# Loading the first chunks of an RWKV-7 scan four steps a partition and turning them by products with the identity

## The chip, the core and the metric

The kernel runs on one core of one Trainium2 chip, as one program from the first load to the last store. The metric is the device time of a run in microseconds, as the median of several runs. A profile comes from one execution of its own; its span is measured from the first to the last recorded instruction.

## What is computed

The input are six tensors of 4 batches, 8 heads, 768 steps and a head dimension of 40. The first part is a recurrence over the steps, with a 40 by 40 state for each batch and head; the second is a dense layer pair over the 3072 resulting tokens of 320 elements.

```python
for t in range(S):
    y[:, :, t] = np.einsum('bhd,bhde->bhe', rt, state)
    Sa = np.einsum('bhde,bhe->bhd', state, at)
    state_decay = state * wt[:, :, None, :] - np.einsum('bhd,bhe->bhde', Sa, bt)
    state = state_decay + np.einsum('bhd,bhe->bhde', vt, kt)
...
h = np.maximum(x @ w_in, 0.0)      # 3072x320 by 320x2048
return h * h @ w_out               # 3072x2048 by 2048x320
```

w lies between 0.85 and 0.95. The dense weights arrive as 64-bit floats and are rounded to 32 bits on the chip. Everything else is 32-bit.

## The kernel before

The steps are cut into chunks of 128, so there are 6 chunks for each of 4 batches, 24 in all, worked chunk by chunk with the four batches of a chunk in turn (`order`). Within a chunk the recurrence is written as products of 128 by 128 matrices per head; only the state passes from one chunk to the next. Heads go in pairs: a head's 40 elements lie padded to 64 rows, so that two heads fill 128 partitions and four pairs (`NP`) fill one PSUM bank of 128 by 512.

**Loading.** `fetch` (L139) brings one of w, a, b, k, r, v of one chunk with one DMA: steps on partitions, 8 heads of 40 elements in each, so 1024 pieces of 160 bytes. It lands in a tile [128, 8, 64] of a ring (L116): two tiles for w, four that a and b share, two each for k and for b as `rest` needs it, one for r, three for v. The pads (elements 40 to 63 of each head) are filled once by POOL, with 1.0 for w and 0.0 for the others (L121). `load_early` (L145) fetches w, b, a of a chunk, `load` (L148) k, the kept decays, r, v and b once more. All of them are issued by SyncE (SP).

**Turning.** `turn` (L313) brings a tile to "elements on partitions, steps along the row", four transposes by TensorE into one bank.

**Early part.** `early` (L342) works on what doesn't need the state. It turns w; scans it on DVE up and down from the middle of the chunk (L352, L353: a running product, `data1` being a tile of ones); takes reciprocals (L357, L358); turns b and a; multiplies them by the decays (L364, L365); stores the decays to memory (`kept_e`); and multiplies b by a for each head (`products`, L320: contraction over the 40 rows). The result N, 128 by 128 for each of 8 heads, is copied by ACT from PSUM into one tile of a single buffer (L373, L376, L377; odd heads are put down with their halves exchanged). It is then stored to memory in pieces: four blocks of the diagonal (`kept_q` or `kept_d`), their joins (`kept_m`, first 10 chunks only) and the off-diagonal quarter (`kept_n`). As there is one buffer for N, the next chunk's first copy waits until these stores have been read out.

**Solve.** The unit triangular matrices 1 + N have to be inverted. POOL does so for the small blocks, in units of 1, 1, 2, 2, 2, 2, 2, 4, 4 and 4 chunks: it loads the kept blocks (L420), solves (L448, L450) and stores the result (`kept_t`, L453). `inverses` (L457) loads the blocks back and joins them to whole inverses with small TensorE products (T copied at L484 to L501).

**Rest and chain.** `rest` (L568) turns k, r and v, and makes the products that the chunk's output needs (A, RV, RX; masked by DVE at L332 with `upper`). `chain` (L604) carries the state through: `xr` (L619), solve by T, the output and the new state. The outputs are the tokens of the dense layers.

**The order of work.** A start-up part does `early` for the first four chunks, of which 0 and 1 keep N on the chip (`g`). Then come 24 slots, one for each chunk. In slots 0 to 3 (`woven`, L881) generators are interleaved by hand-set weights: the chain of the slot, the `rest` of the next chunk, the `early` of up to two later chunks (4 and 5, 6 and 7, 8 and 9, then 10), and the rounding of the dense weights (ACT at L258 and L262, DVE at L266 and others). From slot 4 on (`sorted_slot`, L908) the dense layers fill TensorE, beside the `early`s of chunks 11 and later. Each engine runs its instructions in the order in which the program gave them; an instruction that waits holds up all behind it on that engine. SP issues nearly all DMAs in one such order; `store` (L108) puts a store a few steps behind the place where it is called.

Of the kernel before, what the change touches and what calls it, by code (L numbers as in the profile page):

```python
# [8 lines left out]
FP32 = mybir.dt.float32  # L9
I32 = mybir.dt.int32  # L10
U32 = mybir.dt.uint32
Alu = mybir.AluOpType
# [5 lines left out]
def kernel(  # L18
# [70 lines left out]
    def single(name, shape):  # L89
        return const.tile(shape, FP32, tag=name, name=name)  # L90
# [23 lines left out]


    class Ring:  # L116
        def __init__(self, name, n, shape, fill, pads):
            self.tiles = [single(f"{name}{i}", shape) for i in range(n)]
            self.at = -1
            for t_ in self.tiles:  # L120
                nc.gpsimd.memset(pads(t_), fill)  # L121

        def next(self):
            self.at = (self.at + 1) % len(self.tiles)
            return self.tiles[self.at]

    pads = lambda t_: t_[:, :, D:]
    rings = {}
    for nm, n, fill in (("w", 2, 1.0), ("ab", 4, 0.0)):
        rings[nm] = Ring(f"in_{nm}", n, [128, H, DP], fill, pads)  # L130

    def more_rings():
        for nm in ("k", "b", "r", "v"):
            rings[nm] = Ring(f"in_{nm}", {"r": 1, "v": 3}.get(nm, 2), [128, H, DP], 0.0, pads)

    order = [(bb, c) for c in range(NCH) for bb in range(B)]
    loaded, early_loaded = {}, {}

    def fetch(ring, src, i):  # L139
        bb, c = order[i]  # L140
        t_ = rings[ring].next()
        nc.sync.dma_start(out=t_[:, :, :D], in_=src[bb, :, c * C:(c + 1) * C, :].rearrange("h t d -> t h d"))
        return t_

    def load_early(i):  # L145
        early_loaded[i] = {nm: fetch(ring, src, i) for nm, ring, src in (("w", "w", w), ("b", "ab", b), ("a", "ab", a))}

    def load(i, g=None):  # L148
        x_ = loaded[i] = {"k": fetch("k", k, i)}
# [3 lines left out]
        x_["r"] = fetch("r", r, i)  # L153
        later(lambda: x_.update(v=fetch("v", v, i), b=fetch("b", b, i)), 2 if g is not None else 0)

    load_early(0)
    load_early(1)


    ident = single("ident", [128, 128])  # L160
    make_identity(nc, ident)
    ones = single("ones", [128, MID])
    nc.vector.memset(ones, 1.0)
    upper = single("upper", [128, 128])
    nc.gpsimd.memset(upper, 1.0)
    nc.gpsimd.affine_select(out=upper, in_=upper, compare_op=Alu.is_gt, fill=0.0, base=0,
# [134 lines left out]
    FINE = 6  # L301
    SMALL = units[FINE][0]
    kept_q = dram.tile([SMALL, H, 2, 2, Q, Q], FP32, tag="q", name="kept_q")
    kept_m = [dram.tile([2, Q, H, Q], FP32, tag=f"m{i}", name=f"kept_m{i}") for i in range(SMALL)]
    unit_of = {first + n: u for u, (first, nb) in enumerate(units) for n in range(nb)}

    kept_d = [dram.tile([nb, H, 2, Q * (HC + Q)], FP32, tag=f"d{u}", name=f"kept_d{u}") for u, (_, nb) in enumerate(units)]
# [2 lines left out]
    kept_t = [dram.tile([classes(u), nb, H, 2, 2, Q // classes(u), Q] if u < FINE else [classes(u), nb, H, 2, HC // classes(u), HC], FP32,  # L310
                        tag=f"t{u}", name=f"kept_t{u}") for u, (_, nb) in enumerate(units)]

    def turn(x_):  # L313
        p_ = psum(ps_w)
        for q in range(NP):
            nc.tensor.transpose(p_[:, q * 128:(q + 1) * 128], pair(x_, q), ident)  # L316
        return quads(p_)
# [24 lines left out]
    def early(i, g=None, apart=False):  # L342

        x_ = early_loaded.pop(i)
        dec = decays.next() if g is None else kept_here[i]
        if g is not None:
            nc.vector.memset(dec[:, :A_, :, MID:MID + 1], 1.0)
        up, down, aT = (dec[:, n] for n in (UP, DOWN, A_))
        wT = turn(x_["w"])
        yield  # L350
        for q in range(NP):
            nc.vector.tensor_tensor_scan(up[:, q, MID + 1:C + 1], wT[:, q, MID:], ones, 1.0, Alu.mult, Alu.mult)  # L352
            nc.vector.tensor_tensor_scan(down[:, q, MID - 1::-1], wT[:, q, MID - 1::-1], ones, 1.0, Alu.mult, Alu.mult)  # L353
        yield
        if not apart:
            bT_, aT_ = turn(x_["b"]), turn(x_["a"])
        nc.vector.reciprocal(down[:, :, MID + 1:C + 1], up[:, :, MID + 1:C + 1])  # L357
        nc.vector.reciprocal(up[:, :, :MID], down[:, :, :MID])  # L358
        yield
        if apart:  # L360
            bT_, aT_ = turn(x_["b"]), turn(x_["a"])
            yield
        bT = turned("bT", 1)
        nc.vector.tensor_tensor(bT, bT_, down[:, :, 1:C + 1], Alu.mult)  # L364
        nc.vector.tensor_tensor(aT[:, :, :C], aT_, up[:, :, :C], Alu.mult)  # L365
        if g is None:
            store(kept_e[i], dec[:USED])
        yield
        bb, c = order[i]
        t_ = new("N", [128, H, C], 1)  # L370
        for e, p_ in enumerate(products(bT, aT[:, :, :C])):
            plain, flip_ = t_[:, e:NP:2], t_[:, NP + e::2]
            nc.scalar.copy(plain, p_[:, ::2])  # L373
            for half in range(2):
                own_, other = (slice(n * HC, (n + 1) * HC) for n in (half, 1 - half))
                nc.scalar.copy(flip_[own_, :, own_], p_[other, 1::2, other])  # L376
            nc.scalar.copy(flip_[:HC, :, HC:], p_[:HC, 1::2, HC:])  # L377
        joins = lambda half: t_[half * HC:half * HC + Q, :, half * HC + Q:(half + 1) * HC]
        for half in range(2):
            for n in range(2):  # L380
                at = half * HC + n * Q
                if i < SMALL:
                    kept, to = kept_q[i, :, half, n], at + Q
                else:
                    u = unit_of[i]
                    kept, to = kept_d[u][i - units[u][0], :, half], (half + 1) * HC
                    kept = kept[:, n * Q * HC:n * Q * HC + Q * (to - at)].rearrange("h (s t) -> h s t", s=Q)
                store(kept.rearrange("h s t -> s h t"), t_[at:at + Q, :, at:to], 1, nc.scalar if g is not None and n else nc.sync)
            if i < SMALL and g is None:
                store(kept_m[i][half], joins(half), 1)  # L390
        if g is None:
            store(kept_n[i], t_[:HC, :, HC:], 1)
        else:
            g["dec"], g["N"] = dec, new("N21", [HC, H, HC], 2)
            nc.scalar.copy(g["N"], t_[:HC, :, HC:])
            g["joins"] = spare("joins", i)
            for half in range(2):
                nc.scalar.copy(g["joins"][half * HC:half * HC + Q], joins(half))
        yield
# [57 lines left out]
    def inverses(i, g, queue=nc.sync):  # L457
        bb, c = order[i]
        u = unit_of[i]
        kept = kept_t[u][:, i - units[u][0]]  # L460
        g["T"] = T = new("T", [128, H, HC], 2)
        if u >= FINE:
            for col in range(classes(u)):
                queue.dma_start(out=T[col::classes(u)], in_=kept[col].rearrange("h f j t -> (f j) h t"))  # L464
        else:


            blocks = new("blocks", [128, H, Q], 1)
            for col in range(classes(u)):
                queue.dma_start(out=blocks[col::classes(u)], in_=kept[col].rearrange("h f k j t -> (f k j) h t"))  # L470
        if "N" not in g:
            g["N"] = new("N21", [HC, H, HC], 2)
            queue.dma_start(out=g["N"], in_=kept_n[i])
            if u < FINE:
                g["joins"] = spare("joins", i)
                for half in range(2):
                    queue.dma_start(out=g["joins"][half * HC:half * HC + Q], in_=kept_m[i][half])
        if u >= FINE:
            return
        yield  # L480
        upper_ = spare("turned", i)
        nc.vector.transpose(upper_.rearrange("p h t -> p (h t)"), blocks.rearrange("p h t -> p (h t)"))
        for n in range(2):
            nc.scalar.activation(T[:, :, n * Q:(n + 1) * Q], blocks, Act.Copy, scale=which[:, n:n + 1])  # L484
# [31 lines left out]
    def turn_rv(i, g):  # L516
        x_ = g["x"]
        while "v" not in x_:
            line.pop(0)[1]()
        g["rT"], g["vT"] = turned("rT", 2), turned("kvT", 1)  # L520
        p_, p2_ = turn(x_["r"]), turn(x_["v"])
        nc.scalar.copy(g["rT"], p_)  # L522
        nc.scalar.copy(g["vT"], p2_)
        g["v"] = x_["v"]
# [495 lines left out]
```

## Time and profile before

| what | us |
|---|---|
| median of 3 runs | 987.33 (986.18 to 988.89) |
| the profiled execution, its run | 987.0 |
| its span | 985.3 |
| TensorE busy | 875.7 |
| DVE busy | 485.0 |
| POOL busy | 576.1 |
| ACT busy | 275.5 |
| a turn of four transposes, mean of one transpose record | 0.418 |
| a scan of 128x64 | 0.271 |

The engines work beside each other, so their busy times don't add up to the span. PE is TensorE's matmul side and PEld its weight loads; DVE is VectorE, ACT ScalarE, POOL GpSimd, SP SyncE. A line of the views names the engine, the line of the kernel, the operation and its tiles, output first; in brackets stands the idle time ahead of it on its engine, and what ended that. Matmuls of 32-bit floats show as two records each. The clock given is the share of full speed that TensorE was granted. The DMA share is the mean busy share of the core's 16 DMA engines. The page counts 263431 DMA packets for 104.16 MB, of which 246148 are under 512 bytes.

### The profile page before, as it was taken

To read this page: it belongs to the slowest core of one execution; us is meant where nothing else is said; L and a number is where in the kernel's file an instruction comes from. 1 tells how busy PE (TensorE), PEld (TensorE's weight loads), DVE (VectorE), ACT (ScalarE), POOL (GpSimd) and SP (SyncE) were. 2 spreads that over 40 slices of the span, in tenths; PEclk is the share of its full clock that TensorE was granted. 3 is DMA by queue.
4 is the path that set the end of the run, shared out by engine and by line. 5 is a ranking of instruction groups with operands and counts; after the bars stand their busy time and mean duration, and the time that the engine had idled before them with its cause. 6 is when DMAs were issued, how large, how long until landed. Compare 5 with 4: busy or idle time off the path is not lost.

```text
span 985.3 us, 21632 instructions
## 1 busy us (share of the span) xinstructions
PE 875.7 (89%) x8752; PEld 725.8 (74%) x8752; DVE 485.0 (49%) x868; ACT 275.5 (28%) x711; POOL 576.1 (58%) x989
## 2 busy tenths in 40 slices
PE   6447666667897999999999999999999999999998
PEld 4436555556685888888888888888888888887776
DVE  5528775758755454475446655632444423331111
ACT  3132423234323342332223232322222222222111
POOL 4788482836018985999976999959999800000000
PEclk9757565657698999999999999999999999999999
DMA  8987987894667579465588772585404364030000
GB/s 100 143 160 131 191 158 164 171 170 118 91 127 132 100 138 183 92 122 78 97 167 156 124 113 70 102 183 82 66 19 78 82 121 71 14 64 8 14 13 14
DMA packets 263431, 104.16 MB, mean 106 GB/s; under 512 B 246148, under 2 KB 252676, under 8 KB 261924
## 3 DMA queue, kind: packets, MB, share of 16 engines
q1 hardware_dynamic: 259188, 86.39, 50.9%
q0 software_dynamic: 3056, 16.26, 6.9%
q8 instruction: 69, 1.13, 0.5%
q10 hardware_dynamic: 1088, 0.13, 0.1%
q14 instruction: 30, 0.25, 0.1%
HBM read 70.11 MB, written 30.66 MB: 102 GB/s over the span
## 4 chain that ended last, share of the span: by engine, by line
PE 64%; SPq 1%; DVE 1%; DMA 1%; ACT 0%; issue 0%; ACTq 0%
PE ps_f L87 36%; PE ps_w L87 11%; PE ps_c L87 11%; PE ps_w L316 4%; PE ps_c L560 1%; PE ps_c L643 1%; PE ps_w L544 1%; DMA dec<-kept_e 1%; SPq L108 1%; SPq L464 0%; DMA tokens<-tokens 0%; DVE decay L357 0%; DVE state L535 0%; DVE RV L332 0%; ACT N L376 0%
## 5 line engine op out<-in xcount | busy, mean ns | idle before, releaser
L448 POOL TENSOR_TENSOR half_p<-half_n,half_t 128x120 f32<-128x120 f32 (+37 forms) x438 | 255.7, 584 | 84.4 <-DMA half_n<-kept_d 26.5
L450 POOL TENSOR_TENSOR half_t<-half_t,half_p 128x120 f32<-128x120 f32 (+37 forms) x438 | 275.9, 630 | 34.3
L87 PE MATMUL ps_f<-w_out,hid 128*128 128x320 f32 x768 | 217.4, 436 | 0.0
L87 PEld LDWEIGHTS ps_f<-w_out,hid 128*128 128x128 f32 x768 | 142.5, 190 | 54.6 <-issue 0.2
L87 PE MATMUL ps_f<-tokens,w_in 128*128 128x256 f32 x672 | 157.2, 388 | 0.0
L87 PEld LDWEIGHTS ps_f<-tokens,w_in 128*128 128x128 f32 x672 | 126.7, 194 | 17.9 <-issue 1.0
L734 DVE TENSOR_TENSOR hid<-hid 128x512 f32<-128x512 f32 x96 | 88.9, 963 | 50.2 <-ACT hid L727 49.7
L727 ACT ACTIVATE hid<-ps_f 128x512 f32<-128x512 f32 x84 | 50.2, 597 | 96.0 <-PE ps_f L87 96.0
L352 DVE TENSOR_TENSOR_SCAN decay<-ps_w,ones 128x64 f32<-128x64 f32 x88 | 23.8, 271 | 81.5 <-PE ps_w L316 81.5
L669 DVE TENSOR_TENSOR tokens<-ps_c,dec 128x512 f32<-128x512 f32 x24 | 16.5, 688 | 79.3 <-PE ps_c L87 79.3
L87 PE MATMUL ps_w<-decay,bT 40*128 40x128 f32 x352 | 30.0, 308 | 27.0 <-DVE decay L365 27.0
L373 ACT COPY N<-ps_w 128x256 f32<-128x256 f32 x48 | 17.7, 369 | 121.6 <-PE ps_w L87 74.7
L87 PEld LDWEIGHTS ps_w<-decay,bT 40*128 40x128 f32 x352 | 27.6, 213 | 30.2 <-issue 19.1
L510 DVE TENSOR_TENSOR kvT<-ps_w,dec 128x512 f32<-128x512 f32 x24 | 16.5, 688 | 66.9 <-ACT minus_x L630 33.9
L87 PE MATMUL ps_f<-tokens,w_third 64*128 64x256 f32 x336 | 46.9, 385 | 1.5 <-DVE w_out L266 1.5
L332 DVE TENSOR_TENSOR RX<-ps_w,upper 128x512 f32<-128x512 f32 x48 | 30.8, 683 | 32.1 <-PE ps_w L87 31.6
L332 DVE TENSOR_TENSOR RV<-ps_w,upper 128x512 f32<-128x512 f32 x48 | 30.9, 686 | 31.1 <-PE ps_w L87 30.8
L87 PEld LDWEIGHTS ps_c<-xr,T 64*64 64x64 f32 x768 | 30.7, 149 | 20.5 <-issue 15.0
L522 ACT COPY rT<-ps_w 128x512 f32<-128x512 f32 x24 | 14.0, 585 | 108.3 <-PE ps_w L316 108.3
L87 PE MATMUL ps_c<-xr,T 64*64 64x40 f32 x768 | 36.8, 243 | 3.6 <-ACT xr L619 1.6
L357 DVE RECIPROCAL decay<-decay 128x256 f32<-128x256 f32 x22 | 38.2, 1736 | 0.0
L532 DVE TENSOR_TENSOR f<-end,dec 128x4 f32<-128x4 f32 x20 | 5.1, 255 | 66.6 <-DMA dec<-kept_e 66.6
(130 smaller groups left out, 1411.7 us busy)
## 6 DMA issues: line engine op xcount, KB each, us to landing
kept_e<-decay SPq DMA_DIRECT2D x22, 633.8 KB
dec<-kept_e SPq DMA_DIRECT2D x22, 633.8 KB
hid<-in_moe_w_out_dram SPq DMA_DIRECT2D x16, 320.0 KB
half_n<-kept_d POOLq DMA_DIRECT2D x6, 768.0 KB, 10.3
in_w<-in_w_dram SPq DMA_DIRECT2D x24, 160.0 KB
in_ab<-in_b_dram SPq DMA_DIRECT2D x24, 160.0 KB
in_ab<-in_a_dram SPq DMA_DIRECT2D x24, 160.0 KB
in_k<-in_k_dram SPq DMA_DIRECT2D x24, 160.0 KB
```

Source lines behind the costliest of these rows:

```text
L87: nc.tensor.matmul(o, l_, r_, start=start, stop=True, skip_group_check=True)
L316: nc.tensor.transpose(p_[:, q * 128:(q + 1) * 128], pair(x_, q), ident)
L332: nc.vector.tensor_tensor(t_, p_, over4(upper), Alu.mult)
L352: nc.vector.tensor_tensor_scan(up[:, q, MID + 1:C + 1], wT[:, q, MID:], ones, 1.0, Alu.mult, Alu.mult)
L357: nc.vector.reciprocal(down[:, :, MID + 1:C + 1], up[:, :, MID + 1:C + 1])
L373: nc.scalar.copy(plain, p_[:, ::2])
L448: nc.gpsimd.tensor_tensor(p_, part[:, at:at + m_].unsqueeze(1).to_broadcast([128, n, m_]), t3[:, :n, s:s + 1].to_broadcast([128, n, m_]), ...
L450: nc.gpsimd.tensor_tensor(t3[:, :n, s + 1:], t3[:, :n, s + 1:], p_, Alu.subtract)
L510: nc.vector.tensor_tensor(kT, kT_, down[:, :, 1:C + 1], Alu.mult)
L669: nc.vector.tensor_tensor(t_, y_, g["up"][:, :, :C], Alu.mult)
L727: nc.scalar.activation(h_, p_.rearrange("p f t -> p (f t)"), Act.Relu)
L734: nc.vector.tensor_tensor(h_, h_, h_, Alu.mult)
```

## The change

The w, a and b of chunks 0 to 10 and the r of chunks 0 to 4 are fetched in runs. Four consecutive steps of one head are 160 floats in a row in memory; one partition takes such a run for two heads, in pieces of 640 bytes. The 32 runs of a chunk and one pair of heads fill 32 partitions, and the four pairs the 128, with four DMAs for each fetch. Such a tile is turned by eight products with the identity as the moving operand: for each of the four steps in a run and each head of a pair, 64 columns of the tile are the weight, and the 128 results go to every fourth column of the bank. A weight of 64 columns reads 24 elements past its 40; these belong to the next step, or, at the last, to 24 columns filled by POOL (`beyond`). So the pad rows of a turned tile now hold values of another step. For w the scan therefore takes a second operand `least`, with the larger of the running product and `least` as the result: −3e38 in the rows of the head, 1.0 in its pad rows. The whole pads of such a tile are filled by DVE when the tile is first fetched in the old way. The two first fetches of a are issued by ACT. Beside this, N is laid out [128, 2, 8, 64], by halves of its columns, so that `kept_n` and `kept_m` are stored in pieces of 2048 bytes; `kept_m` becomes twice as large, with the half that is read back as before.

```diff
+    RUN = 4
+    RW = RUN * D
+    flat = lambda t_: t_.rearrange("p h d -> p (h d)")
+    beyond = lambda t_: flat(t_)[:, 2 * RW:2 * RW + DP - D]
+    in_runs = {"w": 11, "ab": 11, "r": B + 1}
...
-        def next(self):
+        def next(self, runs_=False):
             self.at = (self.at + 1) % len(self.tiles)
-            return self.tiles[self.at]
+            t_ = self.tiles[self.at]
+            if not runs_ and self.at in self.bare:
+                self.bare.remove(self.at)
+                nc.vector.memset(self.pads(t_), self.fill)
+            return t_
...
-    def fetch(ring, src, i):
+    def fetch(ring, src, i, queue=nc.sync):
         bb, c = order[i]
-        t_ = rings[ring].next()
+        runs_ = i < in_runs.get(ring, 0)
+        t_ = rings[ring].next(runs_)
+        if runs_:
+            for q in range(NP):
+                queue.dma_start(out=flat(t_)[q * C // RUN:(q + 1) * C // RUN, :2 * RW].rearrange("g (e x) -> g e x", e=2),
+                                in_=src[bb, 2 * q:2 * q + 2, c * C:(c + 1) * C, :].rearrange("e (g s) d -> g e (s d)", s=RUN))
+            return t_
...
-    load_early(0)
-    load_early(1)
+    load_early(0, (nc.sync, nc.sync, nc.scalar))
+    load_early(1, (nc.sync, nc.sync, nc.scalar))
...
-    ones = single("ones", [128, MID])
-    nc.vector.memset(ones, 1.0)
+    least = single("least", [128, MID])
+    nc.gpsimd.memset(least, 1.0)
+    for e in range(2):
+        nc.gpsimd.affine_select(out=least[e * DP:(e + 1) * DP], in_=least[e * DP:(e + 1) * DP], compare_op=Alu.is_ge, fill=-3.0e38,
+                                base=-D, pattern=[[0, MID]], channel_multiplier=1)
...
-    kept_m = [dram.tile([2, Q, H, Q], FP32, tag=f"m{i}", name=f"kept_m{i}") for i in range(SMALL)]
+    kept_m = [dram.tile([2, Q, H, HC], FP32, tag=f"m{i}", name=f"kept_m{i}") for i in range(SMALL)]
...
-    def turn(x_):
+    def turn(x_, runs_=False):
         p_ = psum(ps_w)
+        if runs_:
+            by_step = p_.rearrange("d (x s) -> d s x", s=RUN)
+            for n in range(RUN):
+                for e in range(2):
+                    at = e * RW + n * D
+                    mm(by_step[e * DP:(e + 1) * DP, n], flat(x_)[:, at:at + DP], ident, True)
+            return quads(p_)
         for q in range(NP):
             nc.tensor.transpose(p_[:, q * 128:(q + 1) * 128], pair(x_, q), ident)
         return quads(p_)
...
-        wT = turn(x_["w"])
+        wT = turn(x_["w"], i < in_runs["w"])
         yield
         for q in range(NP):
-            nc.vector.tensor_tensor_scan(up[:, q, MID + 1:C + 1], wT[:, q, MID:], ones, 1.0, Alu.mult, Alu.mult)
-            nc.vector.tensor_tensor_scan(down[:, q, MID - 1::-1], wT[:, q, MID - 1::-1], ones, 1.0, Alu.mult, Alu.mult)
+            nc.vector.tensor_tensor_scan(up[:, q, MID + 1:C + 1], wT[:, q, MID:], least, 1.0, Alu.mult, Alu.max)
+            nc.vector.tensor_tensor_scan(down[:, q, MID - 1::-1], wT[:, q, MID - 1::-1], least, 1.0, Alu.mult, Alu.max)
...
-        t_ = new("N", [128, H, C], 1)
+        t_ = new("N", [128, 2, H, HC], 1)
         for e, p_ in enumerate(products(bT, aT[:, :, :C])):
-            plain, flip_ = t_[:, e:NP:2], t_[:, NP + e::2]
-            nc.scalar.copy(plain, p_[:, ::2])
+            plain, flip_ = t_[:, :, e:NP:2], t_[:, :, NP + e::2]
+            nc.scalar.copy(plain, p_[:, ::2].rearrange("s h (f t) -> s f h t", f=2))
...
-        joins = lambda half: t_[half * HC:half * HC + Q, :, half * HC + Q:(half + 1) * HC]
+        joins = lambda half, f=Q: t_[half * HC:half * HC + Q, half, :, f:]
...
-                store(kept_m[i][half], joins(half), 1)
+                store(kept_m[i][half], joins(half, 0), 1)
         if g is None:
-            store(kept_n[i], t_[:HC, :, HC:], 1)
+            store(kept_n[i], t_[:HC, 1], 1)
...
-                    queue.dma_start(out=g["joins"][half * HC:half * HC + Q], in_=kept_m[i][half])
+                    queue.dma_start(out=g["joins"][half * HC:half * HC + Q], in_=kept_m[i][half, :, :, Q:])
...
-        p_, p2_ = turn(x_["r"]), turn(x_["v"])
+        p_, p2_ = turn(x_["r"], i < in_runs["r"]), turn(x_["v"])
```

More of the change, by code (lines that the diff above doesn't have):

```diff
@@ L116, with __init__ @@
     class Ring:
-        def __init__(self, name, n, shape, fill, pads):
+        def __init__(self, name, n, shape, fill, pads, first=None):
             self.tiles = [single(f"{name}{i}", shape) for i in range(n)]
             self.at = -1
+            self.fill, self.pads = fill, pads
+            self.bare = set(range(n)) if first else set()
             for t_ in self.tiles:
-                nc.gpsimd.memset(pads(t_), fill)
-        def next(self):
+                nc.gpsimd.memset((first or pads)(t_), fill)
@@ L128 @@
+    beyond = lambda t_: flat(t_)[:, 2 * RW:2 * RW + DP - D]
+    in_runs = {"w": 11, "ab": 11, "r": B + 1}
     rings = {}
     for nm, n, fill in (("w", 2, 1.0), ("ab", 4, 0.0)):
-        rings[nm] = Ring(f"in_{nm}", n, [128, H, DP], fill, pads)
+        rings[nm] = Ring(f"in_{nm}", n, [128, H, DP], fill, pads, beyond)
     def more_rings():
         for nm in ("k", "b", "r", "v"):
-            rings[nm] = Ring(f"in_{nm}", {"r": 1, "v": 3}.get(nm, 2), [128, H, DP], 0.0, pads)
+            rings[nm] = Ring(f"in_{nm}", {"r": 1, "v": 3}.get(nm, 2), [128, H, DP], 0.0, pads, beyond if nm in in_runs else None)
@@ L142, in fetch, with load_early @@
         nc.sync.dma_start(out=t_[:, :, :D], in_=src[bb, :, c * C:(c + 1) * C, :].rearrange("h t d -> t h d"))
         return t_
-    def load_early(i):
-        early_loaded[i] = {nm: fetch(ring, src, i) for nm, ring, src in (("w", "w", w), ("b", "ab", b), ("a", "ab", a))}
+    def load_early(i, queues=(nc.sync,) * 3):
+        early_loaded[i] = {nm: fetch(ring, src, i, q) for q, (nm, ring, src) in zip(queues, (("w", "w", w), ("b", "ab", b), ("a", "ab", a)))}
     def load(i, g=None):
@@ L348, in early @@
         up, down, aT = (dec[:, n] for n in (UP, DOWN, A_))
-        wT = turn(x_["w"])
+        wT = turn(x_["w"], i < in_runs["w"])
         yield
         for q in range(NP):
-            nc.vector.tensor_tensor_scan(up[:, q, MID + 1:C + 1], wT[:, q, MID:], ones, 1.0, Alu.mult, Alu.mult)
-            nc.vector.tensor_tensor_scan(down[:, q, MID - 1::-1], wT[:, q, MID - 1::-1], ones, 1.0, Alu.mult, Alu.mult)
+            nc.vector.tensor_tensor_scan(up[:, q, MID + 1:C + 1], wT[:, q, MID:], least, 1.0, Alu.mult, Alu.max)
+            nc.vector.tensor_tensor_scan(down[:, q, MID - 1::-1], wT[:, q, MID - 1::-1], least, 1.0, Alu.mult, Alu.max)
         yield
         if not apart:
-            bT_, aT_ = turn(x_["b"]), turn(x_["a"])
+            bT_, aT_ = turn(x_["b"], i < in_runs["ab"]), turn(x_["a"], i < in_runs["ab"])
         nc.vector.reciprocal(down[:, :, MID + 1:C + 1], up[:, :, MID + 1:C + 1])
@@ L360, in early @@
         if apart:
-            bT_, aT_ = turn(x_["b"]), turn(x_["a"])
+            bT_, aT_ = turn(x_["b"], i < in_runs["ab"]), turn(x_["a"], i < in_runs["ab"])
             yield
@@ L369, in early @@
         bb, c = order[i]
-        t_ = new("N", [128, H, C], 1)
+        t_ = new("N", [128, 2, H, HC], 1)
         for e, p_ in enumerate(products(bT, aT[:, :, :C])):
-            plain, flip_ = t_[:, e:NP:2], t_[:, NP + e::2]
-            nc.scalar.copy(plain, p_[:, ::2])
+            plain, flip_ = t_[:, :, e:NP:2], t_[:, :, NP + e::2]
+            nc.scalar.copy(plain, p_[:, ::2].rearrange("s h (f t) -> s f h t", f=2))
             for half in range(2):
                 own_, other = (slice(n * HC, (n + 1) * HC) for n in (half, 1 - half))
-                nc.scalar.copy(flip_[own_, :, own_], p_[other, 1::2, other])
-            nc.scalar.copy(flip_[:HC, :, HC:], p_[:HC, 1::2, HC:])
-        joins = lambda half: t_[half * HC:half * HC + Q, :, half * HC + Q:(half + 1) * HC]
+                nc.scalar.copy(flip_[own_, half], p_[other, 1::2, other])
+            nc.scalar.copy(flip_[:HC, 1], p_[:HC, 1::2, HC:])
+        joins = lambda half, f=Q: t_[half * HC:half * HC + Q, half, :, f:]
         for half in range(2):
@@ L387, in early @@
                     kept = kept[:, n * Q * HC:n * Q * HC + Q * (to - at)].rearrange("h (s t) -> h s t", s=Q)
-                store(kept.rearrange("h s t -> s h t"), t_[at:at + Q, :, at:to], 1, nc.scalar if g is not None and n else nc.sync)
+                store(kept.rearrange("h s t -> s h t"), t_[at:at + Q, half, :, n * Q:to - half * HC], 1, nc.scalar if g is not None and n else nc.sync)
             if i < SMALL and g is None:
-                store(kept_m[i][half], joins(half), 1)
+                store(kept_m[i][half], joins(half, 0), 1)
         if g is None:
-            store(kept_n[i], t_[:HC, :, HC:], 1)
+            store(kept_n[i], t_[:HC, 1], 1)
         else:
             g["dec"], g["N"] = dec, new("N21", [HC, H, HC], 2)
-            nc.scalar.copy(g["N"], t_[:HC, :, HC:])
+            nc.scalar.copy(g["N"], t_[:HC, 1])
             g["joins"] = spare("joins", i)
```

## The prediction

> **What bounds the kernel now.** I read the slices of the page first, to see which stages have room, then the chain of waits, then a table by stage, then what each stage waits for.
>
> ```profile
> PE   6447666667897999999999999999999999999998
> DVE  5528775758755454475446655632444423331111
> PEclk9757565657698999999999999999999999999999
> DMA  8987987894667579465588772585404364030000
> PE 64%; SPq 1%; DVE 1%; DMA 1%; ACT 0%; issue 0%; ACTq 0%
> ```
>
> A slice is 24.6 us. TensorE is full, at full clock, from about the thirteenth. Before that nothing is full on a compute engine, the clock is at five to seven tenths, and the DMA engines are at eight or nine. The chain that ended last is TensorE for 64%, which reaches back to about 325 us. So an edit pays only if it makes the part before 325 us shorter, or adds TensorE work after it. By stage (the start, then slots 0 to 3 between the first `xr` copies of L619, then slot 4, then the rest):
>
> ```profile
> 0.00:62.00 62.00, 26.80 (x192) 22.04 (x192) 28.26 (x60) 14.74 (x44) 40.53 (x142) 0.80 0.91 126
> 62.00:106.00 44.00, 32.20 (x386) 28.28 (x388) 30.07 (x55) 16.32 (x44) 36.16 (x104) 0.62 0.85 151
> 106.00:156.00 50.00, 32.13 (x347) 28.30 (x344) 37.60 (x67) 17.75 (x45) 26.86 (x76) 0.60 0.88 172
> 156.00:204.00 48.00, 30.86 (x334) 26.84 (x332) 32.00 (x67) 16.02 (x45) 24.67 (x68) 0.57 0.84 166
> 204.00:243.00 39.00, 27.74 (x326) 23.76 (x326) 28.93 (x63) 15.04 (x40) 24.83 (x68) 0.63 0.74 141
> 325.00:986.00 661.00, 656.35 (x6516) 538.58 (x6512) 280.50 (x460) 170.15 (x428) 395.14 (x475) 1.00 0.48 88
> ```
>
> The columns are busy PE, PEld, DVE, ACT and POOL, then clock, DMA share and GB/s. In slots 0 to 3 (181 us) TensorE works 123 us, DVE 129, and no engine is the bound: latency and DMA are. What ends the waits there (total, times, longest):
>
> ```profile
> ACT T L484 <- DMA blocks<-kept_t: 12.3, 3, 6.9
> DVE A L332 <- PE ps_w L87: 10.7, 3, 4.6
> PE ps_w L316 <- DMA in_w<-in_w_dram: 8.9, 3, 4.5
> ACT N L373 <- DMA kept_n<-N: 8.8, 1, 8.8
> PE ps_w L316 <- DMA in_k<-in_k_dram: 6.0, 2, 5.6
> ```
>
> Two of the five are touched directly: the landing of w (8.9) and the release of the N buffer by `kept_n` (8.8). The next lines put them in order of time:
>
> ```profile
> 100.72 0.37 ACT L373 COPY N<-ps_w 128x256 f32<-128x256 f32 x1 [8.77 <-DMA kept_n<-N]
> 117.70 3.47 SPq L142 DMA_DIRECT2D in_w<-in_w_dram  x1
> 125.78 1.08 PE L316 MATMUL ps_w<-ident,in_w 128*128 128x128 f32 x4 [3.25 <-DMA in_w<-in_w_dram]
> 126.80 2.08 PE L87 MATMUL ps_w<-dec,kvT 40*128 40x128 f32 x16
> 128.91 1.29 DVE L332 TENSOR_TENSOR A<-ps_w,upper 128x512 f32<-128x512 f32 x2 [4.59 <-PE ps_w L87]
> 504.66 1.09 PE L87 MATMUL ps_c<-RV,in_k 128*64 128x128 f32 x16
> 515.51 0.60 PE L316 MATMUL ps_w<-ident,in_r 128*128 128x128 f32 x4
> ```
>
> In slot 1 the turn of w stands ahead of the A product in TensorE's order, though that product doesn't need w: the late w holds TensorE, the product holds DVE at L332 for 4.59 us. This is the pattern of slots 1 and 2. The last two lines are the nearest rows for the two ways of turning.
>
> **What the Trainium skill says.** "DMA: Bandwidth & Descriptors", Specifications, gives 512 B as the smallest transfer at line rate. The trace agrees that small pieces are dear: at the start the first four turns begin at 4.16, 5.25, 6.46 and 7.66 us, each released by one fetch of 1024 pieces of 160 B, thus 1.2 us for 164 kB. No piece of 640 B is in the trace. The same page, "Issuing engines are not separate DMA queues", warns that more issuers don't add engines, so the a-fetches put on ACT only spare SP's time. "TensorE: Matmul & The Clock Gate", Part 4, says that a transpose doesn't count as busy time for the clock gate. The trace fits: in 128.90 to 138.40 us TensorE was busy 8.38 of 9.50 us, with transposes and 40-row products, at clock 0.50; the stretches of full clock before 243 us begin after products of 128 rows (in_v with A, RV, RX). Turning by real products may therefore raise the clock.
>
> **The change part by part.** The sum is made against the profiled execution: span 985.3 us, and 987.0 for the run, 1.7 us around it. The median shown is 987.33, 0.3 above that run.
>
> *Fetches.* 38 fetches (w, a, b of chunks 0 to 10; r of 0 to 4) become four DMAs each with 256 pieces of 640 B in place of 1024 of 160 B. The old one costs the engines about 1.15 us. For the new one I take half, 0.55 us, with bounds of 0.3 (a quarter of the pieces, at the old cost of one) and 1.15 (cost by bytes): saved 38 x 0.6 = 23 us of DMA time of about 210 that lie before 243 us. Only what the path waits for counts. Against it stands issue on SP: 114 more DMAs, at some 0.42 us from start to start (small ones such as `kept_q` in this trace), 48 us of queue time in 243. An old fetch took 0.4 us to issue unloaded, 1.2 in a backlog, up to 4.71 in slot 1, and four new ones 1.7. Where there was a backlog they come out even; where there was none they are 1.2 us later. In the built order each hardware DMA also waits for the completion of the one issued eight before it, so eight in flight are now two fetches, not eight: w in slot 1 waits for k, `dec` and r ahead of it. Those lie ahead in the old order too.
>
> *Turns.* Four transposes become eight matmuls with a 64-column weight and 128 columns moving. `RV` by `in_k` has this shape: 504.66 to 505.58, 0.92 us, against 515.51 to 515.95, 0.44, for four transposes; at half clock 1.65 (230.64 to 232.40) against 0.95 (22.37 to 23.25). So +0.5 us warm, +0.7 cold a turn; 38 turns are 20 to 26 us of TensorE, all before 243 us, where it has 100 us idle. The PSUM output has a stride of four; no row has it, and I take it at nothing, with up to +0.5 us a turn as the bound. None of it falls in the full stretch.
>
> *N and its stores.* 22 `kept_n` stores go from 512 pieces of 256 B to 64 of 2048 B, 16 `kept_m` stores from 256 of 128 B to 32 of 2048 B with twice the bytes. The issue on SP (0.56 us) shrinks by about 0.2. What is gone is the end of the 8.77 us wait in slot 0: the product was done at 99.24, so 1.4 us of that wait cost something; then the product is last. The read-back and the ACT copies keep their sizes.
>
> *Scans and pads.* The same 88 scans (271 ns), with `least` for `ones`. Seven DVE memsets of 128x8x24 appear in slots 3 and 4, about 0.2 us each, in DVE's idle (10 of 39 us in slot 3); if uncovered, 1.4 us. POOL's first fills shrink by seven tiles' worth and two selects come in: about even.
>
> *Sum on the path.*
> - Start: w0 is whole 0.35 later (four issues), its turn +0.65 cold, less contention for `half_n` −0.4: +0.6.
> - Slot 0: N copy −1.4; three cold turns ahead of DVE's waits for A, RX and RV +1.3; products at a higher clock −1.5: −1.6.
> - Slot 1: r and w are two cheaper fetches, w lands 1.3 earlier; its turn +0.65; product of 2.08 partly warm −0.45; `blocks` −0.3: −1.4.
> - Slot 2: w −1.0, turn +0.65, clock −0.45 (in_k, 5.55 us at 170.15, is not touched): −0.8.
> - Slot 3: turns +0.5, clock −0.5, store −0.2: −0.2.
> - Slot 4: shorter issue ahead of in_v −0.3. After it nothing.
>
> Together −3.7: span 981.6, run 983.3; from the median 983.6. I take 983.5, 0.39% faster. Of this −2.9 is the clock, the least certain term (0 to −12).
>
> **The rivals.**
> *No change.* For: the largest waits hang on big transfers (`dec`, 633.8 KB, and the weights), w arrives behind them, and the dearer turn eats the rest. Without the clock term and with half the arrival gain: −3.7 + 2.9 + 1.3 = +0.5, thus 985 to 989, around 987.5. Against: the 3.25 and 4.53 us waits for w are the last to end at their places.
> *Slower.* SP is the mechanism: it issues all loads and most stores of a slot in one order, and in slots 0 to 3 three fetches of each `early` and r need 1.2 us more each where the backlog doesn't cover them. With two `early`s a slot, seven such fetches, 8.4 us more per slot on SP; everything behind them, w, `kept_d` and `kept_n`, comes later. It decides when more than some 1.3 us of a slot's extra issue reaches the wait for w; at 2.5 us over what was gained in slots 0 to 2, net +1.2 a slot and the start's +1, it gives +4.6: 992. For: the window of eight is now two fetches deep. Against: issues of 3.47 and 4.71 us show that SP stands waiting in the backlog anyway.
> *Much faster.* If the eight-matmul turns keep the clock up in slots 0 to 3, the products of 40 rows (2.08 us cold) halve in each of some eight places a slot, and slots shrink towards DVE's 30 to 38 us: −3 a slot and −1 for the DMA share, −13: 974. For: cold 0.57 to 0.63 in all four slots. Against: the gaps are filled by waits, not by TensorE, so the clock will fall again.
>
> **How the numbers follow.** Forecast (981 to 986) 0.44; no change 0.23; slower 0.22; much faster 0.11. The range 973 to 992 takes in the clock's bound on one side and SP's on the other; the forecast's own is 981 to 986. About 0.3%, 3.0 us, is what a measurement of this kernel can tell from no change. Faster: three quarters of the first, all of the last, a little of the second: 0.47. Same 0.27, slower 0.26.
>
> **What would show it.** Right: the wait of L316 for in_w falls from 8.9 to about 6 us, the N copy waits for the product and not for `kept_n`, the clock of slots 0 to 3 rises from 0.60 to about 0.65, the stage boundary at 243 comes at about 239.5, and TensorE after 325 us keeps its 656 us. Wrong: waits for in_w or `half_n` grow while SP is busy issuing, turns of over 1.7 us (the stride in PSUM), or more TensorE time in the full stretch.

## The result, and the profile after

The changed kernel takes 997.11 us (median of 4 runs, 995.22 to 1000.49) against 987.74 us (986.18 to 988.89): slower by 1.0%, ratio 1.010 with a 95% interval of 1.0069 to 1.0131. The prediction of 983.5 us, with a range of 973 to 992, is wrong in sign. The profiled execution has a span of 995.2 us, 9.9 more than before.

The first table is the changed kernel's answer by stage, cut where its own stages begin (the first `xr` copies, which are on line 646 there). The columns are those of the prediction's table.

```profile
67.00:109.00 42.00, 32.09 (x478) 28.29 (x480) 30.03 (x56) 16.63 (x45) 33.84 (x99) 0.70 0.72 150
109.00:163.00 54.00, 36.58 (x424) 32.25 (x420) 37.60 (x67) 17.92 (x46) 25.69 (x71) 0.59 0.72 156
163.00:214.50 51.50, 33.95 (x416) 29.58 (x416) 32.12 (x67) 15.96 (x45) 24.69 (x68) 0.63 0.72 163
214.50:253.00 38.50, 29.14 (x373) 25.38 (x374) 29.97 (x67) 15.22 (x41) 23.77 (x65) 0.68 0.71 144
335.00:996.00 661.00, 656.10 (x6513) 538.35 (x6510) 279.19 (x460) 170.09 (x428) 395.96 (x475) 1.00 0.47 88
```

The full stretch of TensorE is what it was: 656.10 busy of 661 us, against 656.35. All of the loss is ahead of it. The DMA engines are less busy than before (0.72 for 0.84 to 0.88), so they are not what got fuller. From the `xr` copies of both traces:

| stretch | before, us | after, us | difference | predicted |
|---|---|---|---|---|
| start, to the landing of slot 0's blocks (T) | 61.5 | 66.8 | +5.3 | +0.6 |
| slot 0, from there | 45.3 | 42.6 | −2.7 | −1.6 |
| slot 1 | 49.3 | 53.6 | +4.2 | −1.4 |
| slot 2 | 48.1 | 51.6 | +3.4 | −0.8 |
| slot 3 | 39.2 | 38.4 | −0.8 | −0.2 |
| slot 4 and the rest | 741.9 | 742.3 | +0.4 | −0.3 |

These are two single executions, and the first two rows are best read together, as +2.6: in e2 and e3 below, whose fetches are those of the kernel before, T lands at 56.9 and 57.9 us, and slot 1 still begins at 106.5 and 108.4.

The waits of the changed kernel from 62 to 253 us that answer to the five of the prediction:

```profile
ACT N L400 <- DMA kept_n<-N: 11.7, 2, 6.6
ACT T L511 <- DMA blocks<-kept_t: 10.7, 2, 8.3
DVE A L359 <- PE ps_w L87: 9.5, 2, 4.8
PE ps_w L87 <- DMA in_w<-in_w_dram: 6.7, 2, 4.3
PE ps_w L343 <- DMA in_k<-in_k_dram: 5.0, 1, 5.0
```

The wait for w has fallen, from 8.9 to 6.7 us, as foreseen. The wait for `kept_n`, which was to go, has grown from 8.8 to 11.7. What tells why is the view of what SP's own queue waited for, here from 0 to 243 us, first of the kernel before:

```profile
SPq L142 <- PE ps_w L316: 15.1, 9, 3.7
SPq L108 <- ACT N L376: 12.0, 3, 7.3
SPq L470 <- DMA kept_t<-half_t: 11.1, 2, 5.9
SPq L108 <- DVE decay L365: 10.6, 2, 7.4
```

and of the changed kernel:

```profile
SPq L108 <- ACT N L403: 10.4, 3, 5.5
SPq L156 <- DMA w_out<-in_moe_w_in_dram: 8.7, 6, 4.7
SPq L156 <- DMA blocks<-kept_t: 4.0, 3, 2.1
SPq L108 <- DMA blocks<-kept_t: 3.3, 1, 3.3
```

Before, SP stood waiting for what the engines had to finish: N, the decays, and the `kept_t` that POOL stores. It was ahead of the work. (The first of its lines is less sure. Those nine waits lie inside SP's own issue records, with no gap ahead of them, so the trace doesn't tell whether SP waited for a free tile or the issue itself took so long.) In the changed kernel three of the four lines are SP waiting for DMAs that were issued earlier and whose data the waiting DMA doesn't use: a fetch waits for a piece of the weights or for the blocks of the inverse. Of the 30 waits for a DMA that SP shows there up to slot 4, 22 are for the one issued exactly eight places before, counted over SP and ACT. SP is behind the work.

The changed kernel's slot 4 begins at 253 us, ten later, and in these ten lies one more wait for an engine, 8.4 us for the decays. Over each kernel up to its own slot 4, the gaps ahead of SP's instructions add up to 35 us before and 20 after for the engines' work, and to 9 and 28 us for the DMA eight places before.

The timeline shows where that reaches the path. Start of the kernel before:

```profile
38.86 3.53 SPq L108 DMA_DIRECT2D kept_e<-decay  x1
54.34 2.61 SPq L470 DMA_DIRECT2D blocks<-kept_t  x4
61.48 0.91 ACT L484 ACTIVATE T<-blocks,which 128x256 f32<-128x256 f32 x2 [8.23 <-DMA blocks<-kept_t]
```

and of the changed kernel:

```profile
41.67 1.91 SPq L156 DMA_DIRECT2D in_w<-in_w_dram  x4
44.09 1.73 SPq L156 DMA_DIRECT2D in_ab<-in_b_dram  x4
45.92 1.77 SPq L156 DMA_DIRECT2D in_ab<-in_a_dram  x4
47.80 0.38 SPq L108 DMA_DIRECT2D kept_e<-decay  x1
54.70 4.15 SPq L497 DMA_DIRECT2D blocks<-kept_t  x4
66.77 0.91 ACT L511 ACTIVATE T<-blocks,which 128x256 f32<-128x256 f32 x2 [8.23 <-DMA kept_q<-N]
```

The first store of chunk 2 is issued by 48.18 and not by 42.39, since the fetches ahead of it are four DMAs each. The four loads of the blocks begin at nearly the same time (54.70 for 54.34), but here they follow straight upon those stores and take 4.15 us to issue for 2.61. T comes 5.3 us later. (Why the loads take 12.1 us from their start to T, and not 7.1, isn't shown.) In slot 1, the kernel before and then the changed one:

```profile
128.31 1.33 SPq L470 DMA_DIRECT2D blocks<-kept_t  x2
138.35 0.45 DVE L482 STREAM_TRANSPOSE spares<-blocks 128x256 f32<-128x256 f32 x1 [1.00 <-DMA blocks<-kept_t]
146.04 0.56 SPq L108 DMA_DIRECT2D kept_n<-N  x1
150.04 0.37 ACT L373 COPY N<-ps_w 128x256 f32<-128x256 f32 x1 [4.85 <-PE ps_w L87]
```

```profile
118.02 7.03 SPq L156 DMA_DIRECT2D in_w<-in_w_dram  x4
134.33 1.35 SPq L497 DMA_DIRECT2D blocks<-kept_t  x2
143.41 0.45 DVE L509 STREAM_TRANSPOSE spares<-blocks 128x256 f32<-128x256 f32 x1 [3.39 <-DMA blocks<-kept_t]
154.46 0.49 SPq L108 DMA_DIRECT2D kept_n<-N  x1
156.86 0.37 ACT L400 COPY N<-ps_w 128x256 f32<-128x256 f32 x1 [6.61 <-DMA kept_n<-N]
```

Measured from the slot's first `xr` copy (106.81 and 109.39), the blocks are issued 3.4 us later, transposed 2.5 us later, and `kept_n` goes out 5.8 us later. N's first copy comes 4.2 us later, at 156.86 for 150.04; before, it was TensorE's product that released it, and in the changed kernel it is `kept_n`. It holds ACT, and the copies of the inverse stand behind it. The slot is 4.2 us longer. Work that is *behind* the fetches in SP's order pays, not the fetch of w.

### The profile page after: what moved, and what is told of

The parts are those of the page before. It is cut to its first block, busy times and chain, and to the rows that moved or that the text cites. A ratio compares the mean times of both kernels' runs of the same rounds, so it can differ in the third digit from the quotient of the medians.

```text
span 995.2 us, 22716 instructions
## 1 busy us (share of the span) xinstructions
PE 888.1 (89%) x9208; PEld 738.8 (74%) x9208; DVE 485.2 (49%) x874; ACT 275.7 (28%) x711; POOL 576.3 (58%) x992
## 4 chain that ended last, share of the span: by engine, by line
PE 66%; ACT 0%; issue 0%; ACTq 0%
PE ps_f L87 37%; PE ps_w L87 11%; PE ps_c L87 11%; PE ps_w L343 4%; PE ps_c L587 1%; PE ps_c L670 1%; PE ps_w L571 1%; ACT hid L754 0%; ACT o L782 0%; ACT minus_x L657 0%; ACTq L782 0%
## 5 line engine op out<-in xcount | busy, mean ns | idle before, releaser
L761 DVE TENSOR_TENSOR hid<-hid 128x512 f32<-128x512 f32 x96 | 86.1, 934 | 50.2 <-ACT hid L754 49.7
L379 DVE TENSOR_TENSOR_SCAN decay<-ps_w,least 128x64 f32<-128x64 f32 x88 | 23.9, 271 | 86.3 <-PE ps_w L343 77.1
L87 PE MATMUL ps_w<-decay,bT 40*128 40x128 f32 x352 | 32.1, 324 | 22.2 <-DVE decay L392 22.2
L559 DVE TENSOR_TENSOR f<-end,dec 128x4 f32<-128x4 f32 x20 | 7.4, 371 | 62.8 <-DMA dec<-kept_e 62.8
```

Of the source, the lines that this page charges most:

```text
L87: nc.tensor.matmul(o, l_, r_, start=start, stop=True, skip_group_check=True)
L761: nc.vector.tensor_tensor(h_, h_, h_, Alu.mult)
```

## The experiments

All times are medians; the kernel before stood beside each at 988.8 to 990.3 us. Ratios are to it, with their 95% interval. The changed kernel's 997.1 us was measured beside 987.7, so a distance from it to a run below is sure to some 1 to 3 us only.

**One part alone.** e1 cuts the old fetch in four, e2 turns by products, e3 lays N out by halves; each is the kernel before in everything else.

```diff
e1:
-        nc.sync.dma_start(out=t_[:, :, :D], in_=src[bb, :, ...]...)
+        cut = 2 if i < in_four.get(ring, 0) else H
+        for h in range(0, H, cut):
+            nc.sync.dma_start(out=t_[:, h:h + cut, :D], in_=src[bb, h:h + cut, ...]...)
e2 (in turn, for w, a, b of chunks 0 to 10 and r of 0 to 4):
+            for h in range(H):
+                q, e = divmod(h, 2)
+                mm(p_[e * DP:(e + 1) * DP, q * 128:(q + 1) * 128], x_[:, h, :], ident, True)
e3: the lines of the change on N, kept_m and kept_n; nothing else
```

> The kernel before with only the 38 fetches each cut into four DMAs of two heads (256 pieces of 160 B); transposes, scans and N as before. If the issue of four DMAs in SP's order (and the window of eight) costs the time, the T of slot 0 comes about 5 us later and the run is 7 to 11 us slower than before (995 to 999). If the dearer turns cost it, this is within 2 us of before (986 to 990).

> The kernel before with only the 38 turns made of eight products with the identity; each fetch is one DMA of 1024 pieces as before. If the dearer turns cost the time, 4 to 9 us slower (992 to 997). If SP's order costs it, within 2 us of before, or up to 3 us faster where the real products raise the clock (985 to 989).

> The kernel before with only N laid out by halves, so that kept_n and kept_m are stored in pieces of 2048 B. If N's stores are held up by SP alone, 0.5 to 2 us faster than before (986 to 987), since N is released earlier in slot 0. If the doubled kept_m or the layout costs something, 1 to 3 us slower (989 to 991).

e1: 1008.8 us, ratio 1.0204 (1.0188 to 1.0219). Cutting the fetches alone costs 20 us, twice the loss of the whole change, and more than expected. At the start, where nothing else is in the way, its fetches move at 79 to 86 GB/s with half of the DMA engines' time busy, those of the kernel before at 136 with nine tenths. A DMA of 41 kB for each 0.47 us of SP's issue (the median) makes 87 GB/s, so by this estimate it is SP's issue that sets their pace. e2: 989.2, ratio 1.0004 (0.9993 to 1.0015): 38 turns by products cost nothing that can be measured, though a cold one takes 1.97 us for 1.1, and the mean clock of slots 1 to 3 rises from 0.60 to 0.66. e3: 987.3, ratio 0.9981 (0.9970 to 0.9991): a gain of about 1.9 us. So neither the turns nor N lose the time; the cut of the fetches into four does, and what the rest of the change gives back takes some half of it away.

**Fewer DMAs a fetch.** e4 and e5 fetch a tile of the change with two DMAs, one for the even and one for the odd heads. They differ in the order of the dimensions. e6 takes runs of eight steps, so that a partition holds one head and one DMA of 128 pieces of 1280 bytes brings the tile; sixteen products of 64 columns turn it.

```diff
e4:
+            for e in range(2):
+                queue.dma_start(out=flat(t_)[:, e * RW:(e + 1) * RW],
+                                in_=src[bb, e::2, ...].rearrange("q (g s) d -> q g (s d)", s=RUN))
e5: as e4, with "q (g s) d -> g q (s d)", and in turn
-            by_step = p_.rearrange("d (x s) -> d s x", s=RUN)
+            by_step = p_.rearrange("d (q g s) -> d s g q", q=NP, s=RUN)
e6 (RUN = 8):
+            queue.dma_start(out=flat(t_)[:, :RW], in_=src[bb, :, ...].rearrange("h (g s) d -> g h (s d)", s=RUN))
...
+            heads = ident.rearrange("p (g q e) -> p e g q", q=NP, e=2)
+                    mm(by_step[e * DP:(e + 1) * DP, n], flat(x_)[:, n * D:n * D + DP], heads[:, e], True)
```

> The changed kernel with two DMAs a fetch in place of four: one for the even and one for the odd heads, 128 pieces of 640 B each; the tile, the turns and N are those of the change. If the number of DMAs in SP's order is the cause, half or more of the loss goes (987 to 992). If the turns are the cause, it stays within 2 us of the changed kernel (995 to 999).

> The changed kernel with two DMAs a fetch, now with partitions in the order run, pair, so that the outermost dimension of a DMA is 32 and not 4 as in e4. If the loss of e4 came from a DMA spread over only a few engines, and the number of DMAs is the cause of the change's loss, a fetch moves at over 120 GB/s and the time is 984 to 990. If something else of the change costs the time, 994 to 998 as in e4.

> Runs of eight steps: partitions in the order run, head, one DMA a fetch with 128 pieces of 1280 B; turned by sixteen products of 64 columns; N as in the change. If the number of DMAs in SP's order is the cause, the loss is gone and the cheaper pieces show: 978 to 985. If the turns by products cost where the fetches are fast, or the fetch in runs itself, 990 to 998.

e4: 995.6 us, ratio 1.0070 (1.0047 to 1.0093), which by its expectation spoke for the turns. The view of the DMA engines (busy tenths and GB/s in 40 slices of the first 60 us) shows another cause; the kernel before, then e4:

```profile
DMA  0799999400164599998999999999976538830259
GB/s 0 124 168 136 136 136 136 37 0 0 22 104 71 147 245 130 131 175 61 173 161 137 136 136 174 158 160 151 161 206 160 78 60 212 242 116 0 44 102 209
```

```profile
DMA  0122222723201646963222313995236922787649
GB/s 0 9 81 90 90 90 90 170 92 76 85 12 22 105 70 167 243 104 106 88 73 39 71 33 101 244 188 106 82 71 142 147 50 88 201 265 193 172 110 214
```

With an outermost dimension of 4 the transfers of e4 keep two tenths of the engines busy and move 90 GB/s, where the old fetch has nine tenths busy at 136. With 32 outermost, e5's first slices reach 205 GB/s, and it takes 984.4 us, ratio 0.9941 (0.9919 to 0.9962). e6 takes 979.6, ratio 0.9890 (0.9859 to 0.9922), the fastest but for its own repeats below, 17.5 us under the changed kernel. It has the change's tiles in runs, turns by products and N, and as many DMAs as before. Its table by stage, for slots 1 to 3:

```profile
105.00:152.50 47.50, 32.55 (x528) 29.64 (x528) 37.49 (x67) 17.67 (x45) 27.49 (x77) 0.68 0.81 183
152.50:197.50 45.00, 31.83 (x528) 28.74 (x528) 32.09 (x67) 15.93 (x45) 24.82 (x68) 0.73 0.74 173
197.50:235.50 38.00, 29.20 (x437) 25.74 (x438) 30.07 (x67) 15.11 (x40) 24.24 (x67) 0.68 0.72 145
```

Slots 1 and 2, 53.6 and 51.6 us in the changed kernel, take 47.8 and 45.0 here, at a clock of 0.68 to 0.73.

**Runs in the start alone.** e7 is the change with `in_runs = {"w": B, "ab": B, "r": 1}`.

> The changed kernel with runs only for w, a, b of chunks 0 to 3 and r of chunk 0, so that the slots fetch as before. If the start's 5 us lateness of T is kept to the end, 990 to 994; if slot 0 has slack for most of it (the change made up 2.7 us there), 987 to 990.

986.1 us, ratio 0.9961 (0.9949 to 0.9973), faster than both expectations allowed. T comes at 57.06 us, not at 66.77. So the start's own fetches in fours do no harm. Up to T the two kernels differ, but for fills of pads by DVE, only in the fetches of chunk 4 and of r of chunk 1, which stand ahead of the stores of chunk 2; that these made T late follows from the order, and no run shows it alone. The loss belongs to what is fetched for the slots.

**Which property of a DMA costs.** e12 cuts e5's two DMAs in two by the runs. e8, e10, e11, e14 and e15 are e6 with DMAs that nobody reads, added to each of the 38 fetches:

```diff
e8:   three, each one piece of 160 B, behind the fetch
+            for _ in range(3):
+                n = len(extra)
+                extra.append(nc.sync.dma_start(out=scratch[n:n + 1], in_=src[bb, 0, n:n + 1, :]))
e10:  three, each sixteen pieces of 20 B, behind the fetch
e11:  as e8, ahead of the fetch
e14:  six as in e8
e15:  as e10, issued by POOL
e12:  e5, with
+            for n in range(2):
+                for e in range(2):
+                    queue.dma_start(out=flat(t_)[n * 64:(n + 1) * 64, e * RW:(e + 1) * RW], ...)
```

> e6 (one DMA a fetch, runs of eight) with three more DMAs on SP behind each of the 38 fetches, each of a single piece of 160 B that nobody reads. 114 DMAs more with 18 kB in all. If the number of DMAs in SP's order is what costs the change its time, whatever they carry, 15 to 20 us slower than e6 (995 to 1000). If it was the shape of the four DMAs (pieces on 32 partitions), within 4 us of e6 (978 to 984).

> As e8, but each of the 114 added DMAs has 16 pieces of 20 B on 16 partitions, so that it can occupy all 16 DMA engines where that of e8 had one piece. If a DMA costs each engine it uses a fixed time beside its bytes, 10 to 17 us slower than e6 (990 to 997). If only SP's order counts, as e8 (982 to 985).

> As e8, but the three added DMAs of one piece stand ahead of each fetch and not behind it, so that the fetch itself waits for what was issued five to eight places before, as the last part of a fetch of the change does. If the wait for the DMA eight places before costs the change its time, 10 to 17 us slower than e6 (990 to 997). If not, as e8 (982 to 985).

> e5 with each of its two DMAs cut in two by the runs: four DMAs a fetch of 64 pieces of 640 B, as in the change, on 64 partitions each, with the outermost dimension 16. If the cut into four costs the time, whatever its shape, as the changed kernel (993 to 998). If it was the change's shape (32 partitions, outermost 32), within 4 us of e5 (981 to 988).

> As e8 with six added DMAs of one piece behind each fetch, 228 in all; at 0.25 us each SP gets about the 60 us of issue that e10 gave it, while each DMA uses one engine. If SP's time decides, as slow as e10 (1000 to 1010). If it is what a DMA costs each of the engines that it uses, twice what e8 cost (985 to 989).

> As e10, with the 114 DMAs of sixteen pieces issued by POOL and not by SP. If they cost the time on the 16 engines, as e10 (1000 to 1010). If they cost it in SP's order, within 5 us of e6 (978 to 986); POOL's own solves can be held up by their issue, so a middling time is POOL's.

e12: 1015.0 us, ratio 1.0248: the cut into four costs 31 us over e5 with the same pieces, the same bytes and another shape than the change's. That is also some 16 to 18 us more than the changed kernel, which neither expectation allowed. With as many DMAs and 64 pieces in each, SP needs 0.59 us to issue one of e12's, over 64 partitions, and 0.43 us for one of the change's, over 32 (medians); so the number of DMAs isn't the whole price. e8: 983.4, only 3.7 over e6, far less than expected; e11: 988.1, between its two expectations, so where the added DMAs stand is worth 4 to 5 us; e10: 1006.9, ratio 1.0170; e14: 1018.3, ratio 1.0282; e15: 995.5, ratio 1.0067 (1.0043 to 1.0091), also between its two.

e8 against e10 made it look as if a DMA cost each of the 16 engines something. The other two rule that out as the main cause. e14's DMAs have one piece each and still cost 39 us, twice as many as in e8 costing ten times as much. e15's have sixteen, and its slots 1 to 3 (from its `xr` copies at 124.74, 172.32, 215.21 and 250.43) take 47.6, 42.9 and 35.2 us, no longer than e6's 47.8, 45.0 and 38.0. Its loss is ahead of them, where POOL issues at 0.48 us apiece between its solves: the first `kept_t` goes out at 58.88 us for e6's 49.02. What e8 and e10 differ in on SP is the issue itself. The line of the added DMAs in e8 and then in e10 (min, median and max in ns):

```profile
L159 SPq DMA_DIRECT2D scratch<-in_w_dram x33: 223/251/832, 1.6 to 186.5; - x33
```

```profile
L159 SPq DMA_DIRECT2D scratch<-in_w_dram x33: 317/424/1956, 1.6 to 200.9; - x33
```

Summed up to the first `xr` copy of slot 4 of each trace, SP's issues, and its waits of over 0.15 us for the DMA eight places before:

| kernel | DMAs on SP | issuing, us | waiting, eight before, us | slot 4 begins, us | run, us |
|---|---|---|---|---|---|
| e6 | 199 | 145 | 13 | 235.6 | 979.6 |
| e5 | 232 | 164 | 11 | 240.3 | 984.4 |
| before | 201 | 181 | 9 | 243.4 | 987.7 |
| e8 | 313 | 175 | 24 | 244.3 | 983.4 |
| e11 | 313 | 178 | 27 | 248.2 | 988.1 |
| changed | 308 | 181 | 28 | 252.9 | 997.1 |
| e12 | 305 | 207 | 18 | 268.4 | 1015.0 |
| e1 | 316 | 201 | 25 | 264.8 | 1008.8 |
| e10 | 315 | 208 | 19 | 262.3 | 1006.9 |
| e14 | 427 | 188 | 50 | 278.6 | 1018.3 |

The rows stand in the order of the two sums together. From e6 to e8 they grow by 41 us and slot 4 comes 9 us later; from e8 to e14 they grow by 39 us more, and slot 4 comes 34 us later. SP has slack at first, and the price begins when it is used up. From e8 to e10 only the issue grows, by 33 us, and the run by 24. The change itself shows the other side, with as much issue as before and 19 us more of waiting. e14 waits most; its longest waits from 0 to 273 us:

```profile
SPq L161 <- DMA dec<-kept_e: 12.6, 3, 4.4
SPq L159 <- DMA w_out<-in_moe_w_in_dram: 9.6, 4, 4.4
SPq L159 <- DMA in_k<-in_k_dram: 8.0, 4, 3.2
```

With seven DMAs to a fetch, SP can't go on past the landing of `dec`, of a piece of the weights or of k. With one DMA to a fetch, in e6, it has no wait for `dec` or k at all.

**SP's time without a DMA.** e9 and its two followers put 24, 60 and 240 empty instructions on SP behind each fetch of e6.

> e6 with 24 empty instructions on SP behind each of the 38 fetches: SP's time without a DMA, so without a place among the eight in flight. If SP's issue time is the cause, slower than e6 by about as much as e8 for the same SP time (seen as the gap behind a fetch in SP's timeline; at about 1.2 us a fetch 990 to 1000). If the wait for the DMA issued eight before is the cause, within 4 us of e6 (978 to 984).

> As e9 with 60 empty instructions on SP behind each of the 38 fetches; e9's 24 left no gap behind a fetch in SP's timeline, so they hid beside the issue or took no time. If SP's time is the cause, slower than e6 in step with the gap that SP's timeline now shows: about nothing for gaps under 0.3 us a fetch, 3 to 10 us for 0.8 us. If it is what a DMA costs the 16 engines or the window of eight, within 3 us of e6 and e9 (978 to 984) whatever the gap.

> As before with 240 empty instructions a fetch. If SP's time is the cause, slower than e6 by about as much as e10 for the same SP time: e10 took 62 us more of SP's time than e6 before slot 4 and 27 us more in all. If it is the 16 engines or the window of eight, within 3 us of e6 (978 to 984) whatever the gap.

981.4, 978.7 and 981.2 us. They decide nothing: the profiled executions of all three show 23772 instructions, as many as e6, so the empty ones are not in them. They are repeats of e6, and say that it is within some 2 us of 980. e10 against e8 shows that SP's issue time costs without more waiting. For the wait for the DMA eight places before there is no such pair, since the changed kernel differs from the kernel before in its pieces, turns and N as well; what a microsecond of it costs stays open.

## Why the prediction was wrong

*What bounds the kernel, and where a change can pay.* Right: the stretch from 325 us kept its 656 us, and all the difference arose ahead of it.

*The step that failed: the fetches.* The prediction named the window of eight and counted 114 more DMAs with 48 us of SP's time, then let them "come out even" where there was a backlog and put both at nothing in the slots of its sum. Alone (e1), the four DMAs cost 20 us. The price of an issue was right (0.43 us for 0.42), and up to slot 4 the changed kernel's issues take no longer in sum than before, 181 us. What it put at nothing is the wait for the DMA eight places before, which went from 9 to 28 us, while SP's waits for the engines fell from 35 to 20: SP had run ahead of the engines, and that lead is what the added DMAs ate. The reading behind the step was that SP stands waiting in the backlog anyway, on the strength of issues of 3.47 and 4.71 us. These are two records of one slot, and a long record doesn't tell what it waited for (of the 4.71 us the profile puts 2.9 down to TensorE still holding the tile); the gaps of the whole stage say the opposite.

*The wait that was watched.* The sum followed w through slots 1 and 2 and gave it −1.3 and −1.0 us. w came earlier in slot 1 (turned 18.2 us after the slot's start for 19.0) and 1.4 us later in slot 2, and the wait for it fell to 6.7 us. What grew was behind it in the same order: blocks, `kept_n`, and in slot 2 k, issued 9.3 us after the slot's start for 5.6.

*The rival.* The slower case named the mechanism, the issue order of SP with its window of eight, and gave it 0.22 and +4.6 us. The sign holds, and the place for slots 1 and 2; slot 0 lost nothing of its own (start and slot 0 together +2.6 us). The size was half of the 9.4 us, because it charged the wait for w alone and at 1.2 us a slot, where slots 1 and 2 lost 4.2 and 3.4.

*The turns.* +0.7 us cold a turn was predicted, 0.9 measured (1.97 for 1.1 us). The prediction's own stretches give that: 230.64 to 232.40 and 22.37 to 23.25 us are 1.76 and 0.88, not 1.65 and 0.95. The stride of four in PSUM costs nothing: e2's turns write without it and take the same 1.97 us cold. The clock term was right in kind: "TensorE: Matmul & The Clock Gate", Part 4, of the Trainium skill says that transposes don't count as busy for the gate, and with real products in their place the mean clock of slots 1 to 3 rose from 0.60 to 0.66 (e2; in e1, without products, it is 0.62). Over all runs the mean clock is 0.910 for e2 and 0.900 for the kernel before (medians of 20 and 39). The prediction's other sign for it holds in part only: of the eight stretches of full clock that begin between 30 and 243 us five come after products of 128 rows, those at 74.8, 115.8 and 221.6 us after products of 64 or 40 rows and turns. In time nothing is left of the dearer turns and the better clock: +0.4 us, not distinguishable from nothing. Whether they cancel or neither reaches the path isn't shown. The much faster rival asked for a clock that stays up; in e2 it rises to 0.66 only, and there is no drop in time. In the changed kernel slot 1 even has 0.59.

*N and its stores.* −1.9 us over slots 0, 3 and 4 was predicted, and −1.9 measured alone (e3, interval −0.9 to −3.0). In the changed kernel it doesn't show, since the release of N hangs there on when SP gets to the store.

*The pieces.* Half the price of a fetch on the DMA engines was a fair estimate: with nearly as many bytes moved, the engines are busy for 38.7 us in place of 43.7 in slot 1 and for 36.9 in place of 40.1 in slot 2, where seven fetches at 0.6 us less make 4.2 (N's stores have a share in it). "DMA: Bandwidth & Descriptors", Specifications, with its 512 B, is borne out in its direction: at nine tenths busy, the start's fetches move at 136 GB/s in pieces of 160 bytes and at up to 300 in pieces of 1280 (e6). With the DMA count unchanged, e6 is 10 us faster than the kernel before, of which N's layout accounts for some 2. The prediction gave the pieces −2.3 us in slots 1 and 2, since it let hardly more than the landing of w gain from them. SP gains too: up to slot 4 it spends 145 us in issue and not 181. How the rest of the 10 us divides between DMA engines and SP isn't shown.

## What to carry to other kernels

Count the DMAs of an issuing queue before their bytes: here cutting a fetch in four cost 20 us where better pieces were worth some 8 (e6, less N's share), and pieces eight times as large brought by one DMA gave a kernel 1.1% faster than before. Ask of such a queue what it waits for: as long as it waits for the engines it has slack, and when it waits for its own earlier DMAs, everything behind it in the order is late. A long issue record alone tells neither. Look behind the transfer that is made faster, at what stands after it in the same queue.

## What the runs showed of the hardware

How many engines a DMA keeps busy went with its outermost dimension: with 4 outermost, the same 640-byte pieces moved at 90 GB/s with two tenths of the engines busy (e4), and reordering the dimensions to 32 outermost took 11 us off the run (e5). What an issue costs SP depends on the shape: 0.25 us for a single piece (e8), 0.42 for sixteen of 20 bytes (e10), 0.43 for 64 pieces over 32 partitions (the change), 0.59 for 64 over 64 partitions (e12). A turn of a tile takes 1.97 us cold and 1.06 at full clock as products of 64-column weights, 1.1 and 0.6 as four transposes, and a stride of four in its PSUM output adds nothing.
